# A transformer block on one core: last residual on GpSimd, transposed chunks spaced, slot loads without a flush

## The chip, the core and the metric

The kernel runs on one core of a Trainium2 chip. The core has five engines with instruction queues of their own: TensorE (PE in the profile; its weight loads are PEld), VectorE (DVE), ScalarE (ACT), GpSimd (POOL) and SyncE (SP), which here only issues transfers. The metric is the device time of one execution in microseconds (us), the median of several runs.

## The reference

One block of a transformer with a condition: S = 2048 rows, D = 448, 16 heads of 28, F = 1792, all in float32.

```
mod = silu(c) @ w_mod                      # six rows of D: sa, ca, ga, sb, cb, gb
h = layernorm(x) * (1 + ca) + sa
q, k, v = split(h @ wqkv)                  # 16 heads
scores = q k^T * 28**-0.5, only where 0 <= i - j < 256
x = x + ga * (softmax(scores) v @ wo)
h = layernorm(x) * (1 + cb) + sb
a = h @ w1 + b1
x = x + gb * (mish(a) @ w2)                # mish(a) = a * tanh(softplus(a))
```

## The kernel before, in words

**Tiling.** The rows are worked on in NG = 4 groups of 512. Every product of a projection keeps its precision by splitting both sides into a high and a low part: a product is 11 matmuls (`passes`), three for each of three chunks of 128 input columns and two for the last chunk of 64. High parts are copies made by ScalarE, low parts are differences made by VectorE or GpSimd.

**Attention.** The unit of work is a slot: one head of one group, slot i = 16 g + head, 64 in all. A slot's q and k rows come from a scratch tensor in device memory, `scr`, written by the stores of the projections (`put` in `qk_out`, lines 322 to 327) and read back by `L` (line 562): one transfer for q, one for k. `A` (line 571) multiplies q and k for the row maxima, which VectorE reduces. `M2` (line 584) transposes the maxima of a pair of slots and writes them into two rows of the q tiles by two small transfers (`q<-mr`). `B` (line 600) multiplies again with these rows included and exponentiates; `SP` (line 625) forms the low part `Pl` on GpSimd; `PV` (line 632) multiplies with v.

**The order.** It is written out by hand, as a loop over units u (line 922), three for each slot s. In unit u the loop runs PV of u - 3 with Pl, B(u), SP(u - 1), then A of slot s + 3 (M2 every second slot), and at k == s % 2 calls `load_slot(s + 5)` (line 943). After that it steps the fillers: generators with the projections of the next group, the output projection of the last one, layernorms and weight preparation. Results of a filler's product pass through `pipe`, whose stages run one unit later each.

**Deferred transfers.** Fillers do not issue their bulk transfers at once but append them to the list `later`: stores of a projection chunk to `scr` (512 and 256 KB each), the loads of the next group's x (`x_load`), of the residual rows (`xr_load`) and of pieces of w_mod and wo. Two places empty it: the unit loop pops one entry in two of a slot's three units (lines 961 and 962), and `flush` (line 304) empties it whole. `load_slot` calls `need` (line 884), which flushes, and, where a chunk that the slot reads is not yet stored (its key is not in `done`), steps the fillers until it is. Some fillers flush too, before they use what they loaded. All transfers go through SyncE's one queue, in program order.

**Feed-forward.** After attention the loop from line 1025 runs over n = 14 g + f, the 56 pairs of a group and a block of 128 hidden columns. An iteration does `f1_mm(n)` (11 matmuls of w1 into bank z), `f1_act(n)` (ScalarE: mish, high part; VectorE: low part `al`), and `ff2(n - 1)` (12 matmuls of w2 into four accumulators). In group 0 it also prepares weights (`pieces`) and runs three fill steps, one ahead of `ff2` and two behind. The filler of group 0 is a chain: `gen_oT(3)` (line 506: the last group's attention output transposed in four chunks), `gen_wo(3)` (its output projection), `finish`, and `gen_x1_ln2(1)`, which calls `gen_ln2` (line 755: layernorm of group 1 and its transposed chunks, `trf`). Each chunk takes one of two "tr" banks. What the filler has not done by n = 14 is drained there. At a group's last block `ff2` multiplies each accumulator with gb (`yo<-acc,gbn`, line 997), adds the residual (line 998) and stores 128 rows.

Of the kernel before, what the change touches and what calls it, by code (L numbers as in the profile page):

```python
# [12 lines left out]
ALU = mybir.AluOpType  # L13

S, D, F, H, DH, W = 2048, 448, 1792, 16, 28, 256
NG, GT = 4, 512
# [35 lines left out]
def adaln_block(ctx: ExitStack, tc: tile.TileContext, x, wqkv, wo, w1, b1, w2, c, w_mod, out):  # L52
    nc = tc.nc
    PE, ACT, DVE, POOL = nc.tensor, nc.scalar, nc.vector, nc.gpsimd
# [3 lines left out]
    def dma(o, i):  # L58
        nc.sync.dma_start(o, i)  # L59
# [25 lines left out]
    def bank(tag, bufs, name):  # L85
        return PS[0].tile([128, 512], F32, name=name, tag=tag, bufs=bufs)
# [14 lines left out]
    for k in range(4):  # L101
        t = st0.tile([112, 2 * D], F32, name=f"wm01_{k}")
# [10 lines left out]
    for part in range(3):  # L113
        for ci in range(4):
            r0, r1 = ci * 128, min(ci * 128 + 128, D)
            for h in ((slice(0, 128),) if ci < 3 else (slice(0, 64), slice(64, 128))):
                t = wqs[ci][h]
# [80 lines left out]
    def gen_ln(tiles, pl, xn_tiles, key, act=False, mv=None):  # L198
        if mv is None:
            mv = pl.tile([128, 4, 2], F32, name=f"mv{key}", tag="mv", bufs=2)  # L200
            for t in range(4):
                ln_stats(tiles[t], mv[:, t, :], pl, f"{key}{t}")
                if t < 3:
                    yield
        rs = pl.tile([128, 4], F32, name=f"rs{key}", tag="rs", bufs=2)
        POOL.tensor_scalar(rs, mv[:, :, 1], EPS, None, op0=ALU.add)
        POOL.tensor_tensor(rs, rs, mhalf, op=ALU.pow)
        yield
        if act:
            nm = pl.tile([128, 4], F32, name=f"nm{key}")  # L210
            POOL.tensor_tensor(nm, mv[:, :, 0], rs, op=ALU.mult)
            POOL.tensor_scalar(nm, nm, -1.0, None, op0=ALU.mult)
        yield
        xs = xn_tiles()
        for t in range(4):
            xn = xs[t]
            if act:
                ACT.activation(xn[:, 0:D], tiles[t], AF.Identity, scale=rs[:, t:t + 1], bias=nm[:, t:t + 1])
                dup(xn)
                yield xs  # L220
                continue
            DVE.tensor_scalar(xn[:, 0:D], tiles[t], mv[:, t, 0:1], rs[:, t:t + 1],
                              op0=ALU.subtract, op1=ALU.mult)
            if t:
                dup(xs[t - 1])
            yield xs
        if not act:
            dup(xs[3])

    def tr_chunk(xs, ci, p):  # L230
        for t in range(4):
            PE.transpose(p[:, t * 128:(t + 1) * 128], xs[t][:, ci * 128:(ci + 1) * 128], ident)
# [5 lines left out]
    def hT_hi(p, ci, hh, si):  # L238
        ACT.activation(hh[:, ci], p, AF.Identity, scale=cols[:, si + 1, ci:ci + 1], bias=cols[:, si, ci:ci + 1])

    def hT_lo(p, ci, hh, hl, si):
        hT_y(p, ci, si)
        DVE.tensor_tensor(hl[:, ci], p, hh[:, ci].bitcast(F32), op=ALU.subtract)

    def new_T(key, pl):
        return (pl.tile([128, 4, GT], F32R, name=f"hh{key}", tag="hh"),
                pl.tile([128, 4, GT], F32R, name=f"hl{key}", tag="hl"))

    V = [(vp if j < 6 else vq).tile([128, H, 60], F32R, name=f"v{j}") for j in range(NV)]
    done = set()  # L250
# [53 lines left out]
    def flush():  # L304
        while later:
            later.pop(0)()
# [123 lines left out]
    for i in range(NK):  # L430
        t = att.tile([86, GT + W], F32R, name=f"k3_{i}")
# [3 lines left out]
    for i in range(2):  # L435
        t = att.tile([128, GT], F32, name=f"o2_{i}")
# [5 lines left out]
    def xr_tile(name):  # L442
        return mid.tile([128, 512], F32, name=name, tag="xr", bufs=3)
# [62 lines left out]
    def gen_oT(g, tag, bufs, oT_pool):  # L506
        o = on[g]
        oh, ol = OT[g] = new_T(f"o{g}", oT_pool)

        def oT_out(p, ci):  # L510
            DVE.tensor_tensor(ol[:, ci], p, oh[:, ci].bitcast(F32), op=ALU.subtract)

        for ci in range(4):
            p = bank(tag, bufs, f"ot{g}{ci}")
            tr_chunk([o[:, t] for t in range(4)], ci, p)
            ACT.activation(oh[:, ci], p, AF.Copy)
            pipe.add(1, lambda p=p, ci=ci: oT_out(p, ci))
            if ci < 3:
                later.append(lambda t=ci: xr_load(g, t))
            yield  # L520

    def xr_load(g, t):
        j = 4 * g + t
        XR[g][t] = xr_tile(f"xr{j}")[:, 0:D]
        dma(XR[g][t], xf[j * 128:(j + 1) * 128, :])
# [154 lines left out]
    w2h, w2l, w2p, h2, x1 = {}, {}, {}, {}, {}  # L680
# [74 lines left out]
    def gen_ln2(g, pl, xn_tiles, tag, bufs):  # L755
        xs = None
        for r in gen_ln([x1[g][:, t, 0:D] for t in range(4)], pl, xn_tiles, f"f{g}", mv=mv2[g]):
            xs = r or xs
            yield 0.6
        hh, hl = h2[g] = new_T(f"f{g}", (mid, FW.get("ff"))[g % 2])  # L760
        for ci in range(4):
            p = bank(tag, bufs, f"trf{g}{ci}")
            tr_chunk(xs, ci, p)
            pipe.add(2, lambda p=p, ci=ci: hT_hi(p, ci, hh, 2), lambda p=p, ci=ci: hT_lo(p, ci, hh, hl, 2))
            yield
            yield

    def gen_ln2_0():
        p1 = FW["p1"]

        yield from gen_ln2(0, p1, lambda: [x1[0][:, t] for t in range(4)], "mm", 2)
        yield from finish()
        for i in range(4):
            piece_load(i)
            yield
# [62 lines left out]
    def fill_main(g):  # L838
        if g == 0:
            yield from gen_qkv(0, VT + (1, 5, 2, 6))  # L840
        else:
            yield from gen_qkv(g, (5, 2, 6))
            while g - 1 not in on_full:
                yield
            yield from gen_oT(g - 1, "mm", 2, mid)
            w1_ready.add(g)
            yield from gen_wo(g - 1, "mm", 2)
        if g + 1 < NG:
            yield from gen_hT(g + 1)
            yield from gen_qkv(g + 1, (0, 3, 4, 1) + VT)  # L850
        else:
            yield from finish()
            yield from gen_ln2_0()
# [28 lines left out]
        return next(fillers[g], 99.0) or RATE[g]  # L882

    def need(keys, g):
        flush()
        while not all((g, m) in done for m in keys):
            pipe.step()
            try:
                next(fillers[max(g - 1, 0)])
            except StopIteration:  # L890
                next(fillers[g])
            flush()

    def load_slot(i):
        if i >= NS:
            return
        g, h = divmod(i, H)
        f0, f1 = h * DH, D + h * DH
        need({f0 // 128, (f0 + 27) // 128, f1 // 128, (f1 + 27) // 128}, g)
        L(i)  # L900

    for i in range(LEAD + 1):
        load_slot(i)
    need({f"v{t}" for t in range(4)}, 0)
    load_slot(LEAD + 1)
    DVE.tensor_copy(identr, ident)
# [15 lines left out]
    for u in range(NU + 9):  # L922
        s, k = divmod(u, 3)
        g = s // H
# [12 lines left out]
        a = s + LEAD  # L937
# [46 lines left out]
    def ff2(n):  # L984
        g, f = divmod(n, NF)
        if f == 0:
            acc[g] = [bank("acc", 4, f"acc{g}_{t}") for t in range(4)]
        for t in range(4):
            ts = slice(t * 128, (t + 1) * 128)
            p = acc[g][t][:, 0:D]  # L990
            PE.matmul(p, ah[n][:, ts], w2h[f], start=(f == 0), stop=False)  # L991
            PE.matmul(p, ah[n][:, ts], w2l[f], start=False, stop=False)  # L992
            PE.matmul(p, al[n][:, ts], w2h[f], start=False, stop=(f == NF - 1))  # L993
            if f == NF - 1:
                j = 4 * g + t
                y = xr_tile(f"yo{j}")[:, 0:D]
                DVE.tensor_tensor(y, p, gbn, op=ALU.mult)
                DVE.tensor_tensor(y, y, x1[g][:, t, 0:D], op=ALU.add)
                dma(of[j * 128:(j + 1) * 128, :], y)

    def gen_x1_ln2(g):
        if g > 1:
            x1_load(g, (ff, p1)[g % 2])
            yield
            yield
            yield

        def xn_tiles():
            t = mid.tile([128, 4, 512], F32, name=f"xn2_{g}", tag="on")
            return [t[:, i] for i in range(4)]  # L1010
        yield from gen_ln2(g, ff, xn_tiles, "tr", 2)
# [13 lines left out]
    for n in range(NN + 1):  # L1025
        g, f = divmod(n, NF)
        if f == 0 and n:
            while fill is not None and next(fill, "END") != "END":
                pipe.step()
            fill = None  # L1030
            while pipe.items:
                pipe.step()
        if f == 2 and 0 < g < NG - 1:
            fill = gen_x1_ln2(g + 1)
        if 2 <= n < NN:
            f1_mm(n, "z")
            f1_act(n)
        if 0 < n < NF:
            pieces(n)
        if n:  # L1040
            fill_step()
            ff2(n - 1)
            for _ in range(1 + (g == 0)):
                fill_step()
# [25 lines left out]
```

## Time and profile before

| what | value |
|---|---|
| time, median of 3 runs | 734.92 us (732.76 to 738.67) |
| the profiled execution's own time | 735.41 us |
| its span, first to last instruction | 733.6 us |
| mean granted TensorE clock | 0.993 |
| PE busy | 692.8 us (94%) |
| DVE busy | 383.1 us (52%) |
| ACT busy | 392.0 us (53%) |
| POOL busy | 326.5 us (45%) |
| moved by DMA | 83.86 MB, mean 114 GB/s |

Attention takes the first 430 us or so of the span, feed-forward the rest. A row of the timeline gives the start, the duration (both in us), the engine, the line, the operation, the tiles (out<-in), shapes and count, and in square brackets how long the engine had been idle and what ended that wait. SPq rows are transfers being issued by SyncE, not their data. Rows of windows give the busy time of each engine in a stretch, the granted TensorE clock (1.00 is full speed), the busy share of the DMA engines and GB/s.

### The profile page before, as it was taken

Reading aid. Unit: us, or ns where it says so; the run is one execution under the profiler, and the core shown is the slowest. Engines: PE = TensorE matmul, PEld = TensorE weight load, DVE = VectorE, ACT = ScalarE, POOL = GpSimd, SP = SyncE. Lnnn points to the kernel's source line nnn. Section 1 sums busy time; section 2 is a strip of 40 time slices with the busy share of each in tenths; the row PEclk is TensorE's granted clock in tenths of the full one; section 3 lists DMA queues with packets and bytes.
Section 4 is the critical chain, followed back from the end, with each engine's and each line's share of the span. In section 5 each row is a group of like instructions: output and inputs, shape, how many; then the busy total and the mean of one; then the engine's idle time right before and its main releaser. Section 6 shows DMA issues by size and latency. Waiting matters only on the chain.

```text
span 733.6 us, 11903 instructions
## 1 busy us (share of the span) xinstructions
PE 692.8 (94%) x3969; PEld 589.6 (80%) x3969; DVE 383.1 (52%) x1014; ACT 392.0 (53%) x740; POOL 326.5 (45%) x358
## 2 busy tenths in 40 slices
PE   3987989999999999999999899999999999999996
PEld 3765767888889888888887678878888888888885
DVE  4858645587865688665667943342324132413113
ACT  3516767776776677767878974343223223322221
POOL 4624788676766586766778953523010000000000
PEclk9999999999999999999999999999999999999999
DMA  8675554365384364462566174400200020001001
GB/s 213 185 249 190 179 158 140 92 204 157 95 263 134 97 205 136 146 197 75 170 206 195 46 239 141 137 13 1 101 0 1 1 100 1 1 0 51 1 0 51
DMA packets 48121, 83.86 MB, mean 114 GB/s; under 512 B 6126, under 2 KB 26108, under 8 KB 48060
## 3 DMA queue, kind: packets, MB, share of 16 engines
q1 hardware_dynamic: 48060, 83.10, 37.5%
q8 instruction: 32, 0.52, 0.3%
q14 instruction: 29, 0.24, 0.1%
HBM read 53.45 MB, written 29.36 MB: 113 GB/s over the span
## 4 chain that ended last, share of the span: by engine, by line
PE 75%; DVE 9%; DMA 6%; ACT 4%; SPq 2%; issue 2%; POOL 1%; DVEq 0%; POOLq 0%; ACTq 0%
PE z L814 20%; PE pv L640 8%; PE qk L294 7%; PE acc L992 6%; PE acc L993 6%; PE acc L991 6%; PE sA L578 5%; PE wo L294 4%; PE sB L608 4%; PE qk_v L294 3%; PE sB L619 3%; DVE junk L580 3%; SPq L59 2%; PE et L651 1%; ACT P L622 1%
## 5 line engine op out<-in xcount | busy, mean ns | idle before, releaser
L630 POOL TENSOR_TENSOR Pl<-P,Ph 128x512 fp32r<-128x512 f32 (+2 forms) x192 | 232.9, 1221 | 84.4 <-ACT Ph L623 50.9
L580 DVE CUSTOM_DVE_ANT_0 junk<-sA,mask 128x384 f32<-128x384 f32 (+2 forms) x256 | 135.3, 529 | 105.2 <-PE sA L578 99.8
L622 ACT ACTIVATE P<-sB 128x512 f32<-128x512 f32 (+2 forms) x192 | 109.8, 572 | 67.7 <-PE sB L619 62.2
L822 DVE TENSOR_TENSOR al<-t,ah 128x512 fp32r<-128x512 f32 x56 | 38.8, 692 | 205.1 <-ACT ah L821 205.1
L820 ACT ACTIVATE t<-z,b1c 128x512 f32<-128x512 f32 x56 | 38.6, 689 | 193.2 <-PE z L814 182.2
L578 PE MATMUL sA<-k,q 84*128 84x384 f32 (+2 forms) x256 | 100.8, 397 | 9.7 <-DVE mx L580 5.4
L623 ACT ACTIVATE Ph<-sB 128x512 fp32r<-128x512 f32 (+2 forms) x192 | 109.3, 569 | 0.0
L814 PE MATMUL z<-hhf,w 128*128 128x512 f32 x224 | 89.4, 399 | 0.0
L814 PE MATMUL z<-hlf,w 128*128 128x512 f32 x224 | 88.8, 396 | 0.0
L991 PE MATMUL acc<-w2h,ah 128*128 128x448 f32 x224 | 82.2, 367 | 0.0
L992 PE MATMUL acc<-w2l,ah 128*128 128x448 f32 x224 | 82.0, 366 | 0.0
L993 PE MATMUL acc<-w2h,al 128*128 128x448 f32 x224 | 81.9, 366 | 0.0
L640 PE MATMUL pv<-Ph,v 128*60 128x256 f32 (+2 forms) x352 | 76.8, 292 | 2.2 <-ACT o L645 2.1
L640 PE MATMUL pv<-Pl,v 128*60 128x256 f32 (+2 forms) x352 | 74.1, 285 | 3.1 <-POOL Pl L630 3.0
L608 PE MATMUL sB<-q,k 86*128 86x256 f32 (+1 forms) x352 | 74.7, 286 | 1.3 <-DMA q<-mr 1.2
L814 PE MATMUL z<-hhf,w1l 128*128 128x512 f32 x168 | 66.3, 395 | 0.0
L608 PEld LDWEIGHTS sB<-q,k 86*128 86x128 f32 x352 | 61.7, 190 | 3.3 <-DMA q<-mr 1.5
L578 PEld LDWEIGHTS sA<-k,q 84*128 84x128 f32 x256 | 49.0, 193 | 18.0 <-DVE mx L580 11.5
L619 PE MATMUL sB<-fdmask,identr 128*128 128x128 bf16 (+1 forms) x320 | 60.3, 254 | 0.0
L640 PEld LDWEIGHTS pv<-Ph,v 128*60 128x60 f32 x352 | 45.6, 133 | 16.6 <-ACT o L645 4.3
L640 PEld LDWEIGHTS pv<-Pl,v 128*60 128x60 f32 x352 | 45.0, 132 | 13.2 <-POOL Pl L630 6.3
L645 ACT ACTIVATE o<-pv 60x512 f32<-60x512 f32 x64 | 37.8, 591 | 24.0 <-PE pv L640 23.2
(149 smaller groups left out, 1257.9 us busy)
## 6 DMA issues: line engine op xcount, KB each, us to landing
scr<-st SPq DMA_DIRECT2D x24, 512.0 KB
k<-scr SPq DMA_DIRECT2D x48, 252.0 KB
q<-scr SPq DMA_DIRECT2D x64, 168.0 KB
scr<-st SPq DMA_DIRECT2D x32, 256.0 KB
x<-x1d SPq DMA_DIRECT2D x10, 448.0 KB
xin<-in_A_x_dram SPq DMA_DIRECT2D x8, 448.0 KB
xr<-in_A_x_dram SPq DMA_DIRECT2D x16, 224.0 KB
x1d<-xr SPq DMA_DIRECT2D x16, 224.0 KB
```

The source lines that it names most:

```text
L294: PE.matmul(p, b, a, start=(n == 0), stop=(n == 10))
L578: PE.matmul(p[:, c0:384], q[0:84, t * 128:(t + 1) * 128], k[0:84, t * 128 + c0:t * 128 + 384], start=True, stop=True)
L580: DVE.tensor_tensor_reduce(out=junk[:, c0:384], in0=p[:, c0:384], in1=mask[:, c0:384], scale=1.0, scalar=-3.0e38, op0=ALU.add, op1=ALU.max ...
L608: PE.matmul(p[:, c:c + 128 * (t1 - t0)], k[:, jj * 128:(jj + 1) * 128], q[:, t0 * 128:t1 * 128], start=(n == 0), stop=False, skip_group_ch ...
L622: ACT.activation(P[:, c0:], p[:, c0:], AF.Exp, scale=SCALE)
L623: ACT.activation(Ph[u][:, c0:], p[:, c0:], AF.Exp, scale=SCALE)
L630: eng.tensor_tensor(Pl[u][:, a:b], Pt[u][:, a:b], Ph[u][:, a:b].bitcast(F32), op=ALU.subtract)
L640: PE.matmul(pv[0:60, t0 * 128:t1 * 128], V[j % NV][:, h, :], P[u][:, c:c + 128 * (t1 - t0)], start=(P is Ph and b == 0 and n == 0), stop=F ...
L814: PE.matmul(zb[n], ps[m][1], ps[m][0], start=(m == 0), stop=(m == 10))
L991: PE.matmul(p, ah[n][:, ts], w2h[f], start=(f == 0), stop=False)
L992: PE.matmul(p, ah[n][:, ts], w2l[f], start=False, stop=False)
L993: PE.matmul(p, al[n][:, ts], w2h[f], start=False, stop=(f == NF - 1))
```

## The change

Three edits, four places:

1. `need` returns at once when all keys of the slot are done. `load_slot` then issues its q and k without emptying `later`; the entries stay for the unit loop's pops or a later flush.
2. `gen_oT` of the last group yields once more behind each chunk, and `gen_ln2` of group 1 yields once ahead of the chunks and once ahead of each. A yield is one fill step.
3. In the last group the residual is added on GpSimd for the first three row tiles; of the fourth, VectorE adds 256 columns and GpSimd the other 192.

```
@@ gen_oT
             if ci < 3:
                 later.append(lambda t=ci: xr_load(g, t))
             yield
+            if g == NG - 1:
+                yield
@@ gen_ln2
         hh, hl = h2[g] = new_T(f"f{g}", (mid, FW.get("ff"))[g % 2])
+        if g == 1:
+            yield
         for ci in range(4):
+            if g == 1:
+                yield
             p = bank(tag, bufs, f"trf{g}{ci}")
@@ need
     def need(keys, g):
+        if all((g, m) in done for m in keys):
+            return
         flush()
@@ ff2
                 DVE.tensor_tensor(y, p, gbn, op=ALU.mult)
-                DVE.tensor_tensor(y, y, x1[g][:, t, 0:D], op=ALU.add)
+                for eng, a, b in (((DVE, 0, D),) if g < NG - 1 else ((POOL, 0, D),) if t < 3 else
+                                  ((DVE, 0, 256), (POOL, 256, D))):
+                    eng.tensor_tensor(y[:, a:b], y[:, a:b], x1[g][:, t, a:b], op=ALU.add)
                 dma(of[j * 128:(j + 1) * 128, :], y)
```

More of the change, by code (lines that the diff above doesn't have):

```diff
@@ L520, in gen_oT @@
             yield
+            if g == NG - 1:
+                yield
     def xr_load(g, t):
@@ L760, in gen_ln2 @@
         hh, hl = h2[g] = new_T(f"f{g}", (mid, FW.get("ff"))[g % 2])
+        if g == 1:
+            yield
         for ci in range(4):
+            if g == 1:
+                yield
             p = bank(tag, bufs, f"trf{g}{ci}")
@@ L884, in need @@
     def need(keys, g):
+        if all((g, m) in done for m in keys):
+            return
         flush()
@@ L997, in ff2 @@
                 DVE.tensor_tensor(y, p, gbn, op=ALU.mult)
-                DVE.tensor_tensor(y, y, x1[g][:, t, 0:D], op=ALU.add)
+                for eng, a, b in (((DVE, 0, D),) if g < NG - 1 else ((POOL, 0, D),) if t < 3 else
+                                  ((DVE, 0, 256), (POOL, 256, D))):
+                    eng.tensor_tensor(y[:, a:b], y[:, a:b], x1[g][:, t, a:b], op=ALU.add)
                 dma(of[j * 128:(j + 1) * 128, :], y)
```

## The prediction, made before the changed kernel ran

> **What bounds the kernel now.** I read the page first, then busy time in 20 us stretches, then TensorE's (PE's) instructions in order of time with the idle time ahead of them.
>
> ```profile
> PE 692.8 (94%) x3969; PEld 589.6 (80%) x3969; DVE 383.1 (52%) x1014; ACT 392.0 (53%) x740; POOL 326.5 (45%) x358
> ...
> PE 75%; DVE 9%; DMA 6%; ACT 4%; SPq 2%; issue 2%; POOL 1%; DVEq 0%; POOLq 0%; ACTq 0%
> ```
>
> By the second line PE carries three quarters of the chain that ends last. It is busy 692.8 of 733.6 us, so the 40.8 us of PE idle time, and what PE loses to its clock, are all that reordering can win. The stretches show where the change can reach (span, then PE, PEld, DVE, ACT, POOL, granted clock, DMA share, GB/s):
>
> ```profile
> 80.00:100.00 20.00, 16.95 (x105) 13.54 (x104) 9.20 (x37) 12.92 (x30) 13.96 (x15) 0.91 0.67 175
> ...
> 460.00:480.00 20.00, 19.32 (x91) 16.48 (x90) 6.77 (x10) 7.08 (x12) 10.26 (x13) 1.00 0.45 128
> 480.00:500.00 20.00, 19.15 (x96) 16.39 (x95) 7.89 (x12) 8.88 (x15) 3.56 (x3) 1.00 0.00 1
> ```
>
> The single waits in them, with what ended each:
>
> ```profile
> 94.48 0.30 PE L578 MATMUL sA<-k,q 84*128 84x128 f32 x1 [3.05 <-DMA k<-scr]
> ...
> 436.77 0.63 PE L232 MATMUL ot<-ident,on 128*128 128x128 f32 x4 [0.73 <-DVE hlo L511]
> ...
> 478.31 0.33 PE L232 MATMUL trf<-ident,xn 128*128 128x128 f32 x1 [0.68 <-DVE xn L222]
> ...
> 484.91 0.63 PE L232 MATMUL trf<-ident,xn 128*128 128x128 f32 x4 [0.85 <-DVE hlf L243]
> ```
>
> The first is a slot load that came late, the other three are transposes in feed-forward group 0 that came too close to what they need. The tail is the third place. All three parts of the change aim at named waits.
>
> **Part 1: slot loads push nothing ahead of themselves.** By the code the wait at 94.48 is A of slot 10 (unit 21, slot 7), whose q and k were loaded at unit 16. At that load the list of deferred transfers held three entries: the first piece of wo, the store of chunk 0 of group 1 (two transfers, 768 KB) and the second piece of wo. need flushed them first. SyncE's queue shows just that:
>
> ```profile
> 83.70 1.43 SPq L59 DMA_DIRECT2D q<-mr  x2
> 85.18 0.45 SPq L59 DMA_DIRECT2D wop<-in_A_wo_dram  x1
> 85.73 0.89 SPq L59 DMA_DIRECT2D scr<-st  x2
> 86.67 0.94 SPq L59 DMA_DIRECT2D wop<-in_A_wo_dram  x1
> 87.71 0.62 SPq L59 DMA_DIRECT2D q<-scr  x1
> 88.38 0.44 SPq L59 DMA_DIRECT2D k<-scr  x1
> 88.86 2.37 SPq L59 DMA_DIRECT2D wop<-in_A_wo_dram  x3
> 91.33 0.51 SPq L59 DMA_DIRECT2D q<-scr  x1
> ...
> 95.33 1.47 SPq L59 DMA_DIRECT2D q<-mr  x2
> ```
>
> Keys of slot 10 were already done, so the new need returns at once: q and k go out at 85.2, wo's first piece and the store follow (units 16 and 17), then slot 11's load, then the other three pieces. Slot 10's k gains 2.5 us of issue and stands ahead of 1.2 MB (224 + 768 + 224 KB by the tiles' shapes); the 3.05 us wait goes. With it goes a stretch at half clock right behind it (these rows: any window, same columns):
>
> ```profile
> 84.00:95.40 11.40, 8.35 (x58) 6.77 (x58) 4.86 (x21) 7.26 (x17) 9.85 (x11) 1.00 0.78 209
> 95.40:98.00 2.60, 2.60 (x13) 2.16 (x12) 1.22 (x5) 0.66 (x2) 1.56 (x2) 0.58 0.08 21
> ...
> 87.17:113.46 26.29, 22.89 (x145) 18.59 (x143) 12.46 (x52) 18.46 (x44) 22.94 (x23) 0.94 0.70 196
> 94.48:100.53 6.05, 6.05 (x31) 5.08 (x31) 2.33 (x10) 2.92 (x7) 2.94 (x4) 0.72 0.52 113
> ```
>
> From 94.48 to 100.53 PE is busy all the time at a mean clock of 0.72: (1 - 0.72) x 6.05 = 1.7 us lost. Wait and clock together are 4.75 us, the upper bound.
>
> Two things are late next. **First the row maxima.** The same bytes now stand between slot 11's load and the q<-mr transfers of slots 8 and 9, and the DMA queue drains only at 95.4 (0.78 busy before, 0.08 behind). Before the change q<-mr was issued at 95.33, held back by the very stall; now its maxima are ready 3.05 us earlier, at 92.3, and it has to follow the bulk.
>
> ```profile
> 55.48 1.53 SPq L59 DMA_DIRECT2D q<-mr  x2
> ...
> 58.28 0.41 PE L608 MATMUL sB<-q,k 86*128 86x384 f32 x1 [0.60 <-DMA q<-mr]
> ...
> 100.53 0.34 PE L608 MATMUL sB<-q,k 86*128 86x384 f32 x1
> ```
>
> With a free queue, PE gets on 1.3 us after the issue's end (57.0 to 58.28); behind a queue that drains at 95.4 I take 1.5 to 2 us, so 97.2. Slot 8's first sB stood at 100.53. Without stall and half clock PE would be there at 95.8; it waits 1.4 us, and the gain is 3.3. **Second POOL.** From 87.17 to 113.46 it multiplies and splits the four pieces of wo beside its attention work and is busy 22.94 of 26.29 us. PE's own work at full clock is 22.89 - 1.7 = 21.2. So POOL becomes the bound of this stretch and no more than 26.29 - 22.94 = 3.35 us can be won. The second piece of wo, now behind slot 11's load, is wanted by POOL here:
>
> ```profile
> 95.08 1.15 POOL L484 TENSOR_TENSOR wop<-wop,ga 128x448 f32<-128x448 f32 x1
> ```
>
> Row 84.00:95.40 has 0.209 x 11.4 = 2.4 MB, moved from about 86.2 (a microsecond behind the first issue) to 95.4, 0.26 MB/us. Of that, 448 KB stand behind the piece, so its bytes are through at 93.6 and it lands a microsecond or two later: POOL waits 0 to 0.6, and what is queued behind it on POOL, the Pl of the next blocks, with it, for which PE's pv waits. I take 0.5. Part 1: 3.3 - 0.5 = **2.8 us**, between 1.1 (a second half-clock stretch, 1.7) and 4.75.
>
> In a sentence apart: the Trainium skill, page TensorE: Matmul & The Clock Gate (section Why this matters for your kernels), says that PE idle gaps of over about 3 us bring the half clock; a gap of 3.05 did so here, and by that rule the 1.4 us left would not.
>
> The other slot loads with a non-empty list (18 in all, by the code's order) change only the order of transfers; there I take 0, covered by the two slots between a load and its first A. Without that cover the price is a wait like the one above.
>
> **Part 2: chunks wider apart.** An extra fill step behind each of the four chunks of gen_oT(3) puts a whole product between the chunks, so the second chunk's copies are done before the third wants the bank: 0.73. In gen_ln2(1) the first transposes now come three steps behind the last xn instead of one, and each chunk one iteration behind the other: 0.68 and 0.85. Sum **2.26 us**; PE's instructions stay the same in number. It costs empty steps: the filler took 28 of 39 steps, now 37. The last chunk's low half is written in iteration 13, behind al on DVE, and is needed by the eleventh matmul of iteration 14. From a later iteration:
>
> ```profile
> 690.08 2.57 PE z L814 x11
> ...
> 695.05 2.56 PE z L814 x11
> ...
> 694.07 0.69 DVE L822 TENSOR_TENSOR al<-t,ah 128x512 fp32r<-128x512 f32 x1 [4.35 <-ACT ah L821]
> ...
> 483.23 0.82 DVE L236 TENSOR_SCALAR trf<-trf,cols 128x512 f32<-128x512 f32 x1
> ...
> 484.07 0.69 DVE L243 TENSOR_TENSOR hlf<-trf,hhf 128x512 fp32r<-128x512 f32 x1
> ```
>
> al ends at 694.76, plus 0.82 and 0.69 is 696.3; the eleventh matmul starts at 695.05 + 10/11 x 2.56 = 697.4. That leaves 1.1 us. If a wait covered the whole tile and not the chunk, PE would stop at the third matmul (695.5) for 0.8 us; that is the lower bound, 1.5.
>
> **Part 3: the tail.** Three adds go to POOL, the fourth is shared.
>
> ```profile
> 725.65 0.62 DVE L997 TENSOR_TENSOR yo<-acc,gbn 128x448 f32<-128x448 f32 x1 [0.97 <-PE acc L993]
> ...
> 727.08 0.37 PE L993 MATMUL acc<-w2h,al 128*128 128x448 f32 x1
> ...
> 729.90 0.62 DVE L998 TENSOR_TENSOR yo<-yo,x 128x448 f32<-128x448 f32 x1
> ```
>
> Now DVE ends at 730.52, then comes the last store. After: products back to back at 725.65, 726.30, 726.95, 727.60. POOL takes 1.15 for such an add (row 95.08) and starts at 726.35: 726.35 + 3 x 1.11 (start to start) = 729.7; 192 columns cost it 0.6, on the line from 0.74 at 256 columns to 1.15 at 448:
>
> ```profile
> 80.83 0.74 POOL L630 TENSOR_TENSOR Pl<-P,Ph 128x256 fp32r<-128x256 f32 x1
> ...
> 423.69 2.32 POOL L630 TENSOR_TENSOR Pl<-P,Ph 128x256 fp32r<-128x256 f32 x2
> ...
> 424.14 0.41 DVE L630 TENSOR_TENSOR Pl<-P,Ph 128x256 fp32r<-128x256 f32 x1
> 424.98 0.44 DVE L630 TENSOR_TENSOR Pl<-P,Ph 128x256 fp32r<-128x256 f32 x1 [0.43 <-issue]
> ```
>
> Two such POOL operations took 2.32 beside two DVE operations on SBUF, where two alone take 1.48: 0.84 more, which is DVE's 0.41 + 0.44. So DVE's half of the last add (0.4) also delays POOL: 729.7 + 0.4 + 0.6 = 730.7, against 730.52. The tail **loses 0.2**, between a gain of 0.3 (no delay) and a loss of 1.3 (POOL held up by the products too). POOL is the new end, not DVE.
>
> The Trainium skill, page SBUF — State Buffer (section Who interferes with whom), has the rule behind that row: a DVE instruction with two SBUF inputs and a GpSimd instruction that reads SBUF hold a shared port exclusively, one with at most one SBUF input does not. By it the products, which read PSUM, are free and the last half add is not; the trace agrees (0.84 against 0.85), and without it the tail would win 0.2.
>
> **Sum.** 2.8 + 2.26 - 0.2 = 4.9 us. The profiled execution took 735.41 (span 733.6, 1.8 around it); that gives 730.5. The median of the runs shown is 734.92, 0.5 lower: **730.0 us**.
>
> **The rivals.**
> *The whole stall is won.* The queue drains sooner once slot loads lead, q<-mr is in time, wo's pieces arrive as POOL wants them, POOL gives no delay in the tail: at most 3.35 by POOL if its work stays, 4.75 if PE runs ahead of it and the lag is made up behind 113; with 2.26 and 0.3 that is 7.3: 727.6. For it: PE has 4.75 us to gain there. Against: the 22.94 us of POOL work.
> *The wait only moves.* q<-mr comes late enough for a new half-clock stretch of 1.7 us: 2.8 - 1.7 + 2.26 - 0.2 = 3.2: 731.8. For it: an idle share and not one gap may set the clock. Against: PE has slack while POOL paces.
> *Slower: the slot load at the head of the queue.* A load issued first can wait for its buffer, and on SyncE's single queue everything behind it (stores, wo, x, row maxima) waits as well; before, the bulk had gone out by then. It acts at the 18 loads that had something to push. From 0.27 us of PE wait at each (4.9 / 18) the gain is gone; at 0.4 it is 7.2 lost, net 2.3: 737.2. For it: PE waits on q<-mr by tenths already at 58.28. Against: the loads in the rows above were issued in 0.4 to 0.6 us, so without such waits.
> *It does not do what it says:* if a key of slot 10 were still in the list, need would flush as before and only 2.1 would be won: 732.8. Against it: by the code's order chunks 2 and 5 of group 0, its keys, were stored before the main loop.
>
> **How the numbers follow.** Forecast 0.50, whole stall 0.14, moved wait 0.22, head of queue 0.10, not done 0.04. A measurement of this kernel can tell about 1% (7.3 us) from no change. Faster by more than that: half of the whole-stall case and a little of the forecast's spread, 0.13. Slower by more: 742 needs 0.7 us at each of 18 loads, 0.03. Within: 0.84. Range: from the whole-stall case less run scatter, 727.0, to the moved wait with POOL's worst tail and scatter, 735.2; left out are most of the slower case and the far end of the first.
>
> **What would show it.** Right: no wait on k<-scr near 91 to 95, q and k of slot 10 directly behind q<-mr at 85; a wait of about 1.4 us on q<-mr at slot 8's first sB and POOL busy nearly throughout 87 to 110; no granted clock under 1.0 there; none of the three transposes' waits; in the tail four DVE products back to back and POOL ending last near the old place. Wrong: a half-clock stretch near 96 to 102, a PE wait on w1 or hlf at iteration 14, waits on loads in groups 1 to 3 that were not there.

## The result, and the profile after

The changed kernel took **729.61 us** (median of 7 runs, 728.66 to 731.82) against 735.71 (7 runs, 732.76 to 738.67) for the kernel before, beside it on the same chip: ratio 0.991, 95% interval 0.989 to 0.993. Measured again, it took 730.24 (6 runs, 728.24 to 731.65) against 734.67 (11 runs): 0.993, 0.990 to 0.995. So 4.4 to 6.1 us were won. The forecast was 4.9 won, 730.0 us.

The profiled execution took 728.97 us, span 727.2, mean granted clock 0.989. From its page, the busy time of each engine, and the shares of the chain that ended last:

```profile
PE 690.9 (95%) x3969; PEld 588.4 (81%) x3969; DVE 381.4 (52%) x1011; ACT 392.3 (54%) x740; POOL 331.2 (46%) x362
...
PE 69%; issue 11%; DVE 8%; ACT 5%; DMA 4%; POOL 2%; SPq 1%; POOLq 0%; DVEq 0%; ACTq 0%
```

PE's busy time fell by only 1.9 us while the span fell by 6.4: what went is idle time, as intended. POOL took over 4.7 us, with four more instructions.

**Where the 6.4 us came from.** Both kernels run the same PE instructions, so one instruction that stands in both shows how far one execution is ahead at that point. Before the change (start, duration, engine, line; the last matmul is the row at 727.08 in the prediction):

```profile
81.87 0.68 PE L640 MATMUL pv<-Ph,v 128*60 128x384 f32 x1
...
124.92 0.37 PE L294 MATMUL qk_v<-wql,hh 128*128 128x448 f32 x1
...
427.49 0.40 PE L640 MATMUL pv<-Ph,v 128*60 128x256 f32 x2
```

The same three after it, and the last matmul:

```profile
80.28 0.69 PE L642 MATMUL pv<-Ph,v 128*60 128x384 f32 x1
...
120.91 0.37 PE L294 MATMUL qk_v<-wql,hh 128*128 128x448 f32 x1
...
423.31 0.40 PE L642 MATMUL pv<-Ph,v 128*60 128x256 f32 x2
...
720.06 0.36 PE L1001 MATMUL acc<-w2h,al 128*128 128x448 f32 x1
```

The lead is 1.59 us at the first row, 4.01 at the second, 4.18 at the third, 7.02 at the last matmul and 6.4 at the end. So 1.59 came ahead of part 1's place, 2.4 in it, 0.2 in the rest of attention, 2.84 in feed-forward, and the tail lost 0.62. The 1.59 belong to the execution and not to the change: the first slot load that the change moves in SyncE's order comes behind the q<-mr pair of row 55.48, and that pair already goes out 1.83 us earlier (53.65). Without the 1.59, 4.8 us are left.

**Part 1 in the profile.** SyncE's queue after the change:

```profile
82.12 1.60 SPq L59 DMA_DIRECT2D q<-mr  x2
83.81 0.41 SPq L59 DMA_DIRECT2D q<-scr  x1
84.27 0.38 SPq L59 DMA_DIRECT2D k<-scr  x1
84.70 0.37 SPq L59 DMA_DIRECT2D wop<-in_A_wo_dram  x1
85.18 0.89 SPq L59 DMA_DIRECT2D scr<-st  x2
86.16 1.10 SPq L59 DMA_DIRECT2D q<-scr  x1
87.31 0.91 SPq L59 DMA_DIRECT2D k<-scr  x1
88.26 2.98 SPq L59 DMA_DIRECT2D wop<-in_A_wo_dram  x4
91.80 1.46 SPq L59 DMA_DIRECT2D q<-mr  x2
```

Slot 10's q and k go out directly behind q<-mr, then wo's first piece, the store, slot 11's load and the rest of wo: the order that the prediction gave. Its A no longer waits. What waits in its place, by the view of PE's waits between 85 and 112 us (total, times, longest):

```profile
PE pv L642 <- POOL Pl L632: 3.0, 6, 0.8
```

And the stretch in which POOL does its attention work and wo's pieces, between the same two instructions as row 87.17:113.46 of before (the row ends 0.07 us short of the second, which starts at 109.82), with the place in feed-forward below it:

```profile
85.60:109.75 24.15, 21.79 (x145) 17.05 (x142) 12.45 (x52) 18.29 (x43) 22.96 (x23) 1.00 0.73 224
...
426.00:500.00 74.00, 74.00 (x362) 64.34 (x361) 25.15 (x41) 33.18 (x58) 28.91 (x31) 1.00 0.38 114
```

POOL does the same 22.96 us of work (22.94 before) in 24.2 instead of 26.29 us: it has become the bound there, and PE waits for its Pl six times. (The last two of the six, 1.0 us together, stand in the profile of before too.) The wait for q<-mr of 1.4 us that the prediction put at slot 8's first sB is not in this execution, though the transfers were issued behind the bulk (91.80 above): that product starts at 95.10 with no wait of 0.15 us or more ahead of it. What POOL itself waits for:

```profile
89.49 1.15 POOL L484 TENSOR_TENSOR wop<-wop,ga 128x448 f32<-128x448 f32 x1 [1.00 <-PE pv L642]
...
94.69 1.14 POOL L484 TENSOR_TENSOR wop<-wop,ga 128x448 f32<-128x448 f32 x1
```

It waits 1.00 us at the first piece of wo (the trace names a PE instruction that had long ended; the piece was issued at 84.70, behind slot 10's load, and by the trace's packet records its last packet ended at 88.68), and not at all for the second, where the prediction had looked.

**Part 2.** Row 426:500 shows PE without any gap in feed-forward group 0. The same stretch of before had 2.26 us of idle time, the three bubbles of the prediction:

```profile
426.00:500.00 74.00, 71.74 (x352) 61.44 (x350) 27.78 (x48) 34.93 (x62) 28.09 (x31) 1.00 0.41 123
```

**Part 3.** The tail after the change, beside the last matmul (720.06, end 720.42):

```profile
718.62 1.85 DVE L1005 TENSOR_TENSOR yo<-acc,gbn 128x448 f32<-128x448 f32 x3 [0.96 <-PE acc L1001]
719.33 3.33 POOL L1008 TENSOR_TENSOR yo<-yo,x 128x448 f32<-128x448 f32 x3 [107.99 <-DVE yo L1005]
...
722.56 0.62 DVE L1005 TENSOR_TENSOR yo<-acc,gbn 128x448 f32<-128x448 f32 x1 [2.09 <-DMA out_dram<-yo]
723.22 0.42 DVE L1008 TENSOR_TENSOR yo<-yo,x 128x256 f32<-128x256 f32 x1
723.26 0.83 POOL L1008 TENSOR_TENSOR yo<-yo,x 128x192 f32<-128x192 f32 x1 [0.61 <-DVE yo L1005]
```

Three products run back to back, the fourth does not: it writes a `yo` tile, of which there are three (`xr_tile`, tag "xr", bufs=3), and the first one is still being stored. That store is issued only at 720.51, when POOL has ended its first add, and DVE waits 2.09 us for it. The last add ends at 724.09, 3.67 us behind the last matmul; before it was 730.52 - 727.45 = 3.07.

### The profile page after: what moved, and what is told of

The parts are those of the page before. It is cut to its first block, busy times and chain, and to the rows that moved or that the text cites. A ratio compares the mean times of both kernels' runs of the same rounds, so it can differ in the third digit from the quotient of the medians.

```text
span 727.2 us, 11903 instructions
## 1 busy us (share of the span) xinstructions
PE 690.9 (95%) x3969; PEld 588.4 (81%) x3969; DVE 381.4 (52%) x1011; ACT 392.3 (54%) x740; POOL 331.2 (46%) x362
## 4 chain that ended last, share of the span: by engine, by line
PE 69%; issue 11%; DVE 8%; ACT 5%; DMA 4%; POOL 2%; SPq 1%; POOLq 0%; DVEq 0%; ACTq 0%
PE z L820 15%; PE pv L642 8%; PE qk L294 7%; PE qk_v L294 5%; PE acc L1000 5%; PE acc L1001 5%; PE acc L999 5%; PE sA L580 4%; PE wo L294 4%; PE sB L610 4%; PE sB L621 3%; DVE junk L582 3%; ACT P L624 2%; PE et L653 1%; DMA wm<-in_w_mod_dram 1%
## 5 line engine op out<-in xcount | busy, mean ns | idle before, releaser
L1008 POOL TENSOR_TENSOR yo<-yo,x 128x448 f32<-128x448 f32 (+1 forms) x4 | 4.2, 1060 | 108.6 <-DVE yo L1005 108.6
```

## The experiments

Each part alone first, then the disputed places. The tables count by the four PE instructions above: part 1's place is from the first to the second, the rest of attention from the second to the third, feed-forward from there to the last matmul, the tail from its start to the end of the span (6.52 us before). All are us won against the profile of before.

**e1: part 1 alone.**

```
     def need(keys, g):
+        if all((g, m) in done for m in keys):
+            return
         flush()
```

> Before, with the early return of need alone. Theory POOL: the 3.05 us wait on slot 10's k and the half clock behind it go, but POOL, which multiplies and splits the four pieces of wo, paces PE between about 85 and 110 us; PE waits on Pl several times there (3 us in sum), and 2.0 to 2.5 us are won in all. Rival queue (as predicted): PE waits some 1.4 us on q<-mr at slot 8's first sB, and 2.8 are won. Rival whole stall: no such waits, 4.75 won.

Measured: 731.89 us against 734.68 (0.997, 0.995 to 0.999), 2.8 less. Its profile, of the longest of the 12 executions (735.98), shows both kinds of wait:

```profile
91.65 1.13 POOL L484 TENSOR_TENSOR wop<-wop,ga 128x448 f32<-128x448 f32 x1 [1.81 <-DMA wop<-in_A_wo_dram]
...
93.53 0.33 PE L640 MATMUL pv<-Pl,v 128*60 128x256 f32 x1 [1.53 <-POOL Pl L630]
97.58 0.41 PE L608 MATMUL sB<-q,k 86*128 86x384 f32 x1 [0.16 <-DMA q<-mr]
```

POOL waits 1.81 us for wo's first piece, PE then waits 1.53 us for Pl four microseconds ahead of the place where it was to wait for q<-mr, and that second wait is 0.16. When POOL has held PE back, the row maxima are hardly late. The waits are those of the expectation's first theory, the 2.8 us of the time are the rival's figure; one profile, and of the longest execution, can't decide between them.

**e2: part 2 alone.** The yields of `gen_oT` and `gen_ln2`, nothing else.

> Before, with the extra fill steps alone. Theory pitch: the idle time of a row counts from the modelled end of a pipelined matmul, which is later than the next one could have started, so the three waits (0.73, 0.68, 0.85) cost more than they show, about 2.85 us won in feed-forward group 0. Rival: the listed waits are the whole cost, 2.26 won.

Measured: 731.87 against 734.68 (0.996, 0.994 to 0.998), 2.8 less. Feed-forward won 2.90 us between the two instructions, with PE busy through the whole stretch:

```profile
426.00:500.00 74.00, 74.00 (x362) 64.15 (x361) 25.30 (x44) 34.69 (x61) 29.05 (x31) 1.00 0.40 122
```

So the part is worth 2.9 us, as expected here, and not the 2.26 of idle time.

**e3: part 3 alone.** The additions of the last group on GpSimd, as in the change.

> Before, with the last group's residual on GpSimd alone. Theory buffer: the fourth product writes a buffer that the first output is still being stored from (three buffers), so it waits about 2 us for that store; from the end of the last acc matmul to the end of the last add 3.7 us instead of 3.07, 0.6 us slower. Rival lock (as predicted): products back to back, 0.2 slower.

Measured: 735.32 against 734.68 (1.000, 0.998 to 1.002): no difference in the time can be told. The profile can tell it: the tail is 0.68 us longer, and the fourth product waits for a store here too.

```profile
730.31 0.62 DVE L997 TENSOR_TENSOR yo<-acc,gbn 128x448 f32<-128x448 f32 x1 [2.08 <-DMA out_dram<-yo]
```

**e4: the change without part 3.**

> The changed kernel with the residual of the last group back on VectorE. Theory buffer: 0.6 us faster than the changed kernel, 6.7 us faster than before by the profiles (tail of 3.07 us behind the last matmul). Rival lock: 0.2 faster than the changed kernel.

Measured: 730.25 against 734.68 (0.993, 0.990 to 0.995). Not to be told from the changed kernel by its time; by its profile the tail is at 6.52 us again, 0.6 less than with part 3.

**e5: six buffers for the last group's sums.**

```
-                y = xr_tile(f"yo{j}")[:, 0:D]
+                y = (xr_tile if g < NG - 1 else stage)(f"yo{j}")[:, 0:D]
```

> The changed kernel with the last group's four outputs in staging tiles of six buffers instead of three. Theory buffer: the fourth product no longer waits for the store of the first (2.09 us), the four products run back to back, and from the end of the last acc matmul to the end of the last add it takes 2.8 (no hindrance between DVE's half add and POOL) to 3.3 us (the half add holds POOL up by 0.4), against 3.66; 0.4 to 0.8 us won. Rival: POOL's adds alone set the end and nothing changes, 3.66.

Measured: 730.94 against 735.61 (0.993, 0.991 to 0.996), and the tail:

```profile
721.59 2.46 DVE L1005 TENSOR_TENSOR yo<-acc,gbn 128x448 f32<-128x448 f32 x4 [0.96 <-PE acc L1001]
...
724.08 0.74 DVE L1008 TENSOR_TENSOR yo<-yo,x 128x256 f32<-128x256 f32 x1
```

```profile
722.29 4.06 POOL L1008 TENSOR_TENSOR yo<-yo,x 128x448 f32<-128x448 f32 x4 [107.99 <-DVE yo L1005]
```

Now four products in a row, and POOL's four additions without a pause. The wait for the store is gone, and with it 0.7 us: the last add ends 2.97 us behind the last matmul (723.38 to 726.35). The buffer was the cause. The time alone can't show so small a gain. What is left is a hold-up between the two engines: DVE's half add takes 0.74 beside POOL instead of 0.42, and POOL is the last to end.

**e6: the same buffers, two additions on each engine.** GpSimd adds tiles 0 and 1, VectorE tiles 2 and 3.

> As the one with staging tiles, and the adds shared as two row tiles on POOL and two on DVE. Theory lock: adds of two SBUF operands on the two engines follow each other, so the end is 0.7 + 2 x 1.11 + 2 x 0.6 behind the first product, 2.2 to 2.5 us behind the last matmul against 3.66: 1.2 to 1.5 us won over the changed kernel, 0.6 to 0.9 over the old tail. Rival: they overlap freely, and then 1.9 us.

Measured: 730.21 against 735.61 (0.993, 0.991 to 0.996); from the last matmul (end 722.51) to the last add 2.82 us, more than the 2.2 to 2.5 that were expected.

```profile
722.60 1.54 DVE L1007 TENSOR_TENSOR yo<-yo,x 128x448 f32<-128x448 f32 x1
724.06 0.61 DVE L1005 TENSOR_TENSOR yo<-acc,gbn 128x448 f32<-128x448 f32 x1
724.71 0.62 DVE L1007 TENSOR_TENSOR yo<-yo,x 128x448 f32<-128x448 f32 x1
```

The third tile's add stands ahead of the fourth product in DVE's order. Beside POOL's adds it takes 1.54 instead of 0.62 us, and the product waits behind it.

**e8: wo's first piece ahead of slot 10's load.**

```
     def load_slot(i):
         if i >= NS:
             return
+        if i == LEAD + 7 and later:
+            later.pop(0)()
```

> The changed kernel with the first entry of the list sent ahead of slot 10's load (the first piece of wo). Theory POOL: POOL's 1.0 us of waiting for that piece ends, and since POOL paces the stretch to 110, all after it comes about 1.0 us earlier; slot 10's k lands 0.7 to 0.9 us later and is still in time. Rival: slot 10's A waits on k again and the microsecond is lost there.

Measured: 729.64 against 735.61 (0.993, 0.990 to 0.995). POOL's wait is gone, and a wait on q<-mr comes up:

```profile
88.69 1.15 POOL L484 TENSOR_TENSOR wop<-wop,ga 128x448 f32<-128x448 f32 x1
```

```profile
95.38 0.41 PE L610 MATMUL sB<-q,k 86*128 86x384 f32 x1 [0.77 <-DMA q<-mr]
```

The time can't be told from the changed kernel's, and this profile does not show what the edit did: in three executions without it (again, e4 and e5, below) POOL does not wait for that piece either.

**e9: that, and the four multiplications of wo's pieces by ga on VectorE,** which takes 4 x 1.15 us off POOL.

> As the one before, and the four multiplications of wo's pieces by ga on VectorE instead of GpSimd. Theory POOL: POOL loses 4 x 1.15 us of work, PE's waits on Pl between 85 and 112 (3.0 us in sum in the changed kernel) nearly vanish, and 2 to 3 us are won over the changed kernel. Rival lock: four DVE operations with two SBUF operands hold POOL up (0.6 each) and delay the row maxima, and less than 1 us is won beyond the first piece's microsecond.

Measured: 729.48 against 735.61 (0.992, 0.989 to 0.995). Every wait on Pl in the stretch is gone, as expected; in its place:

```profile
97.87 0.41 PE L610 MATMUL sB<-q,k 86*128 86x384 f32 x1 [1.78 <-DMA q<-mr]
```

Both of the prediction's next bounds are there: with POOL's taken away, the wait on q<-mr is left. That it grows as POOL is relieved (0.16 in e1, 0.77 in e8, 1.78 here) is not shown, since with all of POOL's work it was 1.51 to 1.72 in three executions and absent in two. The 2 to 3 us over the changed kernel that were expected did not come: part 1's place won 4.22, against 2.43 on the mean of five profiles with the change's loads and POOL work, and the time can't be told from the changed kernel's.

**e10: that, without the emptying of the list ahead of the four pieces** (one `flush()` in `gen_mod_wo` taken out).

> The kernel with the first piece of wo popped early and its four multiplications by ga on DVE, less the emptying of the list ahead of the four pieces, so that their loads go out one by one at the later pops. Theory queue (the 1.78 us that slot 8's first sB waited for q<-mr are the bulk transfers that stand ahead of it in SP's order): fewer loads ahead of it, the wait falls to 0.9 us or less, and the time is 0.5 to 1 us under the same kernel with the emptying, 729.48. Rival, POOL or DVE now paces the stretch: the wait falls, but an idle time of the same size comes up at pv on Pl or at DVE's multiplications on wop, and the time stays.

Measured: 728.89 against 734.67 (0.992, 0.989 to 0.994). The expectation missed. The transfers leave in the same order as in e9, the last pieces of wo still ahead of q<-mr, and PE waits 2.16 us for it:

```profile
88.72 1.61 SPq L59 DMA_DIRECT2D wop<-in_A_wo_dram  x3
90.50 1.46 SPq L59 DMA_DIRECT2D q<-mr  x2
```

The unit loop's own pops had sent them by then; the emptying had nothing left to send. So the run repeats e9, and whether fewer bytes ahead of q<-mr shorten the wait has not been tried.

**e11: e10 with a mended tail.** Six buffers, POOL adds tiles 0 and 1, and the additions of tiles 2 and 3 come on DVE behind the fourth product.

```
+                ys[t] = y
+                for i in ((), (2, 3))[t == 3] if g == NG - 1 and t > 1 else (t,):
+                    eng = POOL if g == NG - 1 and t < 2 else DVE
+                    eng.tensor_tensor(ys[i], ys[i], x1[g][:, i, 0:D], op=ALU.add)
+                    dma(of[(4 * g + i) * 128:(4 * g + i + 1) * 128, :], ys[i])
```

> The same with the last group's sums in the six-buffer tiles, the additions of tiles 0 and 1 on GpSimd, those of tiles 2 and 3 on VectorE behind the fourth product. Theory (the tail lost its 0.6 us to the buffer, and then to the addition that stood ahead of the fourth product): the fourth product starts within 0.1 us of the last matmul's end, and from there to the end of the last addition are 2.0 to 2.4 us instead of 3.66; the time is 1 to 2 us under the changed kernel's. Rival (the lock of the two engines costs what the order wins): 2.8 us or more.

Measured: **727.07** against 734.67 (0.990, 0.987 to 0.992), the fastest median here, 3.2 us under the changed kernel beside it (1 to 2 were expected) and 1.8 under e10, from which it differs in the tail alone; the intervals of all three still overlap. The tail did as expected:

```profile
716.92 2.46 DVE L1007 TENSOR_TENSOR yo<-acc,gbn 128x448 f32<-128x448 f32 x4 [0.96 <-PE acc L1003]
...
717.63 2.24 POOL L1011 TENSOR_TENSOR yo<-yo,x 128x448 f32<-128x448 f32 x2 [107.99 <-DVE yo L1007]
...
718.35 0.36 PE L1003 MATMUL acc<-w2h,al 128*128 128x448 f32 x1
719.29 1.59 DVE L1011 TENSOR_TENSOR yo<-yo,x 128x448 f32<-128x448 f32 x2
```

From the last matmul's end, 718.71, to the last add's, 720.88, are 2.17 us: 1.5 less than in the changed kernel, 0.9 less than before it.

**The changed kernel once more.**

> The changed kernel once more beside the two, for a comparison on one chip: 729 to 731 us, 0.990 to 0.994 of before.

Measured: 730.24 against 734.67, as told above. Its profile differs from the first one above all in the disputed place, and once more near 406:

```profile
97.58 0.41 PE L610 MATMUL sB<-q,k 86*128 86x384 f32 x1 [1.72 <-DMA q<-mr]
...
406.33 0.47 PE L610 MATMUL sB<-q,k 86*128 86x384 f32 x2 [0.84 <-DMA q<-mr]
```

```profile
94.59:98.00 3.41, 1.69 (x11) 1.05 (x9) 0.39 (x2) 1.85 (x4) 3.10 (x4) 1.00 0.75 194
98.00:101.42 3.42, 3.42 (x14) 2.73 (x13) 1.71 (x7) 1.78 (x5) 2.67 (x4) 0.50 0.94 244
```

Here PE waits 1.72 us for q<-mr at slot 8's first sB, and a stretch at half clock follows. POOL does not wait for wo's first piece, the waits on Pl shrink to one of 0.59, and POOL's stretch, from 87.12 to 111.59, takes 24.5 instead of 24.2 us for the same work.

**Which wait shows.** Two rows of other runs, e6 and e4, show the same two kinds of execution:

```profile
91.06 1.14 POOL L484 TENSOR_TENSOR wop<-wop,ga 128x448 f32<-128x448 f32 x1 [0.60 <-DMA wop<-in_A_wo_dram]
```

```profile
96.32 0.41 PE L610 MATMUL sB<-q,k 86*128 86x384 f32 x1 [1.51 <-DMA q<-mr]
```

Six profiles have slot 10's load and POOL's work as the change has them. In three of them POOL waits for wo's first piece (after 1.00, e6 0.60, e1 1.81 us), and PE waits 0 to 0.16 for q<-mr. In the other three (again, e4, e5) POOL does not wait, and PE waits 1.5 to 1.7 us. SyncE issues the same transfers in the same order in all six, but they land at different times. By the packet records the first piece's last packet ended 3.96 to 5.01 us behind the start of its issue in the first three, and 3.13 to 3.35 in the others. The last packet of q<-mr ended 0.73 us behind the end of its issue in after and e6, and 2.1 to 2.8 in the other four.

**All profiles side by side** (us won against the profile of before; POOL's wo work and the tail as in the change unless the row says otherwise):

| profile | ahead of part 1's place | part 1's place | rest of attention | feed-forward | tail | waits in part 1's place | late in attention |
|---|---|---|---|---|---|---|---|
| after | 1.59 | 2.43 | 0.16 | 2.84 | -0.62 | Pl 3.0 | |
| after, again | 0.06 | 2.08 | -0.66 | 2.86 | -0.64 | q<-mr 1.72, half clock, Pl 0.59 | q<-mr 0.84 |
| e4 (old tail) | 1.15 | 3.32 | -1.34 | 2.76 | 0.00 | q<-mr 1.51, Pl 0.99 | half clock |
| e5 (six buffers) | 0.42 | 1.67 | -0.90 | 2.87 | 0.04 | q<-mr 0.42 and 1.59, half clock, Pl 0.61 | q<-mr 0.95 |
| e6 (two and two) | -0.36 | 2.67 | -0.23 | 2.85 | 0.27 | Pl 2.7 | |
| e1 (part 1 alone) | 0.23 | 1.74 | -2.60 | 0.05 | -0.03 | Pl 3.5, q<-mr 0.16 | q<-mr 0.80, half clock |
| e2 (part 2 alone) | 1.06 | -0.85 | 0.36 | 2.90 | 0.03 | k<-scr; half clock 93 to 100 | |
| e3 (part 3 alone) | 0.46 | 0.01 | -1.29 | 0.09 | -0.68 | k<-scr, as before | half clock |
| e8 | 1.36 | 3.53 | 0.36 | 2.85 | -0.60 | q<-mr 0.77, Pl 1.5 | |
| e9 | -0.14 | 4.22 | -1.61 | 2.81 | -0.58 | q<-mr 1.78 | q<-mr 1.33 |
| e10 | 2.02 | 4.04 | -0.63 | 2.86 | -0.59 | q<-mr 2.16 | q<-mr 0.79 |
| e11 | 0.91 | 4.60 | 0.35 | 2.86 | 0.67 | q<-mr 1.58 | |

Feed-forward and tail repeat within 0.15 us. Part 1's place scatters by 1.7 us among kernels with the same attention, the rest of attention by 1.5, and the start by 2. The last column sorts the rest of attention. Profiles with neither entry lie between -0.23 and 0.36. A stretch of 3.41 us at half clock (granted 0.50, from 418.41 in e4 and from 422.40 in e3) comes with a loss of 1.3; e3 has the old slot loads, so this is no effect of the change. A wait on q<-mr near 405 (in e1, e5 and e9 with a smaller one besides) comes with losses of 0.6 to 1.6; where it comes from is told in the last section.

## Why the prediction was right

The total was right: 730.0 forecast, 729.61 and 730.24 measured. By its steps:

- **The slot load (right).** The wait of 3.05 us on k<-scr and the half clock behind it went, and the transfers left in the order that was given.
- **What is late next (both named; which one shows changes with the execution).** The wait on q<-mr was forecast at 1.4 us. Of five profiles with the changed attention and slot 10's load as in the change (after, again, e4, e5, e6) three have it, at 1.72, 1.51 and 1.59, and two have none. POOL was forecast as the bound of the stretch, and those two show it alone, with 3.0 and 2.7 us of waits on Pl. The prediction took both at once; where POOL comes late first, it hides the wait on q<-mr. Part 1's place won 2.43 us on the mean of the five ((2.43 + 2.08 + 3.32 + 1.67 + 2.67) / 5), against 2.8.
- **Which piece of wo (wrong).** The prediction's 0.5 us for POOL was a wait of 0 to 0.6 for the second piece; that wait was 0.30 us at most (again). Where POOL did wait longer, by 0.60 to 1.81 us in three of six profiles, it was for the first piece, which stood ahead of slot 10's load before and behind it now. In the other three the first piece was in time. What sending it first is worth is not shown: e8 won 3.53 us in the place, e4 won 3.32 without that edit and without the wait.
- **No new half clock (right in three of five).** The rival of the moved wait, a new stretch at half clock for 1.7 us, is what "again" and e5 show. Their place won 2.08 and 1.67 us. e4, the one of the five with the same wait at full clock, won 3.32: 1.24 and 1.65 more (e5 has a second wait of 0.42 besides). By these three single profiles the half clock cost about its price, and the slack that the prediction held against this rival does not show.
- **Part 2 (mechanism right, size too small).** The term was 2.26 us, the sum of the listed idle times; the gain was 2.76 to 2.90 in the ten profiles that have the part, 2.85 on their mean. The listed idle time begins at the modelled end of a matmul, and in a stream the next one starts well before that end. By the groups of instructions of the changed kernel (min, median and max of one, in ns) a transpose takes 272 ns:

```profile
L232 PE MATMUL ot<-ident,on x64: 270/272/327, 150.0 to 440.0; 128*128 128x128 f32 x64
```

Four in a row take 0.60 to 0.63 us (row 436.77), so they follow each other at 0.11. At a stop PE is counted as busy for those 0.16 us that it would not have needed. The time from start to start holds them: in the profile of before the three rows start 1.01, 0.95 and 1.21 us behind the matmul ahead of them, where 0.11, 0.11 and 0.20 would have done (0.20 is the pitch of the acc matmuls). That is 2.75 of the 2.85; the last 0.1 is not accounted for.
- **Part 3 (sign right, size and cause wrong).** The step that failed is "products back to back at 725.65, 726.30, 726.95, 727.60": the fourth had to wait for a tile. The term was a loss of 0.2; it was 0.62 to 0.68, of which the buffer is 0.7 (e5). With six buffers the order of the forecast comes out, 2.97 us from the last matmul to the last add where its arithmetic gives 730.7 - 727.45 = 3.25. The 0.4 by which DVE's half add was to hold POOL up went the other way: POOL's four adds take 4.06 us, 3 x 1.11 and 0.73, and it is DVE's half add that takes longer.
- **Slower by the head of the queue (not seen at its price).** The rest of attention stands 0.7 us behind on the mean of the ten profiles with the new slot loads. Part of it is the half clock in e1 and e4, which e3 has with the old loads. The rest is the wait on q<-mr near 405, which five of the ten have (again, e1, e5, e9, e10): by the table some 0.5 us on the mean of the ten, an estimate, where the prediction took 0. None of the three profiles with the old loads has it, but it hangs on a few hundredths of a microsecond (last section), and nothing ties it to the order of the slot loads: SyncE issues the same transfers in the same order there. All of it is far from the 7.2 us of the rival.

In sum 2.43 + 2.85 - 0.63 = 4.65 us against 4.9: two terms were too kind and one not kind enough, and that they cancel is luck. The two measurements of the gain, 6.1 and 4.4 us, have intervals that overlap, and single executions scatter by 2 us in the start alone.

Of the two rules that the prediction weighed: the Trainium skill, page TensorE: Matmul & The Clock Gate (section Why this matters for your kernels), would keep the full clock through gaps under about 3 us. The runs disagree: "again" got half clock behind a longest gap of 1.72 us, and the kernel before got it with no gap over 0.9, while e10 kept full clock through one of 2.16 (rows below). The Trainium skill, page SBUF — State Buffer (section Who interferes with whom), has a DVE instruction with two SBUF inputs and a GpSimd instruction that reads SBUF shut each other out. The trace agrees: e5 (0.74 instead of 0.42) and e6 (1.54 instead of 0.62) show it, and so do the products, which read PSUM and keep their 0.62 beside POOL.

## What to carry to other kernels

When work is moved to another engine to free the first, count the buffers between them: an add that ends later holds its tile longer, and the next producer waits for the store behind it. When a queue is reordered, look at what the displaced transfer feeds and at the engine that paces the stretch; here both next waits were real, and an early one hid the later. For stops in a stream of matmuls take the time from start to start, not the listed idle time. And take more than one profile of a kernel before a wait is called its cost: the two of the changed kernel show different waits in the same place.

## What the runs showed of the hardware

**The half clock comes in pieces of about 3.41 us, or two of them (6.83 us in e2, 93.09 to 99.92), and neither the idle share nor the longest gap decides alone.** In e10, the stretch ahead of and behind its 2.16 us gap:

```profile
92.15:95.56 3.41, 1.75 (x11) 1.16 (x10) 2.07 (x5) 2.33 (x5) 3.41 (x4) 1.00 0.72 186
95.56:98.98 3.42, 2.92 (x20) 2.49 (x20) 2.01 (x8) 1.72 (x5) 1.99 (x3) 1.00 0.95 232
```

PE was busy 1.75 of 3.41 us and kept full clock (the gap, 93.90 to 96.06, runs over the edge at 95.56, so 1.66 us of it lie in the first piece); in "again" it was busy 1.69 of 3.41 and lost half. In the profile of before, a piece with 1.96 of 3.40 busy was followed by one at half:

```profile
48.00:51.40 3.40, 1.96 (x8) 1.07 (x8) 2.91 (x11) 0.60 (x1) 0.79 (x2) 1.00 0.31 118
51.40:54.90 3.50, 3.50 (x11) 2.52 (x10) 2.91 (x8) 0.00 (x0) 1.19 (x4) 0.51 0.91 311
```

Where in the program these pieces lie differs from one execution to the next: four of the changed kernel's relatives have one near 98 or near 420, the first profile has neither. That is part of the scatter in the table; what decides is left open.

**A few packets decide when a small transfer lands.** A q<-mr pair is 16 packets of 512 bytes in the packet records. With a drained queue the last one ended 0.74 us behind the end of the issue (before, 96.80 to 97.54). In the first profile of the changed kernel it took 0.73 too (93.26 to 93.99), though packets of wo, issued ahead of it, still started up to 95.18. In the second profile fourteen packets were through at 95.34 and the last two at 96.36. PE went on 1.1 to 1.4 us behind the last packet in all eight profiles in which it waited there. What held the last packets back in this place is not shown.

**One packet behind an instruction transfer is the wait near 405.** Beside the kernel's own transfers every execution has 32 packets of 16 KB on a queue that the profile calls "instruction". In the five profiles with the wait on q<-mr one such packet came in between: in "again" it took from 404.06 to 405.02, fifteen of the pair's packets were through by 404.45, and the sixteenth ended at 405.08. In all five the sixteenth ended 0.02 to 0.07 us behind the 16 KB packet, 1.3 to 1.9 us behind the issue; in the eight other profiles all sixteen were through in 0.73 or 0.74. The five 16 KB packets started 1.71 to 1.75 us behind the start of the pair's issue, those of the others 1.78 us or more behind it, or ahead of it.
